# Block 1's first product wholly by seven half products, under a new hand-written order

## The chip, the cores and the metric

The kernel runs on one core of one Trainium2 chip. The metric is the device time of one launch in microseconds (us), lower is better. The core's engines are named as in the profile: PE is TensorE's matrix multiplication and PEld its weight loads, DVE is VectorE, ACT is ScalarE, POOL is GpSimd (here it only issues loads), and SP is SyncE (here it issues transposing DMAs and stores).

## The reference, cut to what matters

Attention with a window feeds a two-layer network. There are 4 batches of 768 tokens, that is 24 tiles of 128 tokens, 8 heads of 64.

```python
scores = scale * q @ k.T + bias            # 96 local keys and 8 global keys are kept
a = softmax(where(keep, scores, -1e9))
x = (a @ v) laid out as 3072 tokens x 512
h = x @ w_in                               # "first product",  512 -> 2048
g = maximum(h, 0) ** 2
out = g @ w_out                            # "second product", 2048 -> 512
```

## The kernel before, in words

The 24 tiles make 12 blocks of two tiles. Tiles 0 and 1 are block 0, tiles 2 and 3 block 1, and so on. For a tile j the program records named operations: the load of q, k and v (`ld.q.j`, `ld.k.j`, `ld.v.j` for the first six tiles, `load.j` later; all issued by POOL in `swdge`, L327), the transposes of q and k on PE (`tr.0.j`, `tr.1.j`) with their copies out of PSUM (`T.0.j`, `T.1.j`), the scores (`sc.j`, after `bias.j` for tiles 0 to 2), the exponentials (`exp.j.odd.g`, ACT), the product with the bias table (`mul.j.g`, DVE), the product with v (`pv.j.half`, PE), its division (`norm.j.half`, two DVE instructions), and the transpose of x (`trx.j` on PE and a copy `xT.j` for tiles 0 to 7, a transposing DMA on SP from tile 8). `gk`, `gv` copy the global keys and values into the tile's own buffers; `gate.j` is a tiny DVE write that a load waits for.

The network's first product for a block has 8 steps of 256 hidden columns. It stands in the program in two forms:

- Plain (`s1.blk.s`, `emit_s1` at L1074): 8 matrix multiplications of 256 columns for one step (in block 0 some steps are cut by token tile or column half), then `relu.blk.s` and `sq.blk.s`.
- By seven half products (`first_seven`, L917; this is the scheme by which a 2x2 block product takes seven block products and some sums, not eight products). Four steps form a group; a group has the products `h.blk.g.p1` to `p7`, each of 8 matrix multiplications of 128 columns. Their operands are parts of `w_in` and of x, sums of parts of `w_in` (`isum.i.g`, four for each group, made once, DVE, L907) and sums of parts of x (`xs.blk.0..2`, DVE, L939). Between products in one PSUM bank the partial results are copied out (`u.blk.g.1..3`). Three of the four quarters of the hidden block come from an addition with relu on DVE (`c.blk.g.c11`, `c12`, `c22`, L1011), and one, `c21`, from a plain relu. Four squares `q.blk.g.*` follow.

The second product goes by seven half products in every block (`s2`, with `sum` and `wsum` on DVE, `part` copies and `o` additions).

Block 0's first product is plain; blocks 2 to 11 go by seven (`SEVEN1`, L280); of block 1 the second group alone goes by seven (`SEVEN1_PART`, L281), and the steps 0 to 3 are plain.

The sums of `w_in` are written over the buffers of the first tiles' q and k (`first_sum`, L238), so each `isum` waits for every transpose and bias product of the tiles 0 to 5 (`first_reads`) and for the four steps of `w_in` that it reads.

Each engine runs its instructions in order. What that order is, and which PSUM bank or buffer each operation takes, is written out by hand in the string `ORDER` (L57), which `Plan.run` (L39) reads word by word: `name:banks`, with `@A` or `@V` where ACT or DVE may do the operation and `#2` for a second one of that name. The order of the loads (words `ld.` and `load.`) is POOL's, that of `T.j` (from tile 8), `xT.j` (from tile 8) and `st` is SP's.

Of the kernel before, what the change touches and what calls it, by code (L numbers as in the profile page):

```python
# [62 lines left out]
trx.1:6 exp.3.0.1 exp.3.1.0:7 exp.3.0.0 ld.win.1.0 pv.2.0:2 pv.2.1:5 norm.2.0:0 norm.2.1 gv.2@V mul.3.0:8 sc.4.0:1037
exp.4.1.0:9 trx.2:2 ld.win.4.0 xT.1@A exp.4.1.1:a tr.1.5:4 tr.0.5:5 T.1.5@A exp.4.0.0 xT.2@A:1 mul.3.1:b pv.3.0:0
pv.3.1:6 T.0.5@A s1.0.1:7 norm.3.0:1 gk.4@V exp.4.0.1 norm.3.1 gv.3@A s1.0.1#2 trx.3:4 sc.5.0:0126 exp.5.0.1:c
exp.5.1.0:d s1.0.4:5 exp.5.1.1 E0.0 mul.4.0:e xT.3@V ld.v.4 mul.4.1:f ones.6 pv.4.0:3 s1.1.1:4 relu.0.4@V:2 exp.5.0.0
ld.win.3.0 s1.0.3:2 pv.4.1:1 relu.0.1@A:0 sq.0.1@A:0 gv.4@A s1.0.3#2 mul.5.1:1 s1.1.3:6 norm.4.0:0 norm.4.1 ld.win.2.0
ld.win.0.0 s1.0.0:5 relu.0.3@A:3 sq.0.3@A mul.5.0:5 gate.10 s1.0.2:0 trx.4:7 relu.1.1@A:4 sq.1.1@A:1 xs.1.0:0 ld.v.5
ld.win.2.1 pv.5.0:3 ld.win.0.1 pv.5.1:1 xs.1.1 ld.win.6.0 ld.win.7.0 ld.win.5.0 relu.1.3@A:7 norm.5.0:1 norm.5.1
ld.wout.3 s1.1.2:2 xT.4@A:2 relu.1.2@A:8 ld.wout.2 ld.wout.1 ld.wout.0 isum.0.0 s1.1.0:4 s1.0.2#2 trx.5:3 gate.14  # L70
xT.5@V relu.1.0@A:6 sq.1.2@A s1.0.0#2 xs.2.0:1 h.2.0.p1:1 sq.1.0@V sq.0.4@A u.2.0.1@A:b isum.3.0 sq.1.3@A xs.2.1
ld.wout.7 isum.0.1 s1.0.0#3 s1.0.6:6 gate.11 isum.1.0 isum.1.1 xs.1.2 s1.0.7:7 h.2.0.p2:2 c.2.0.c11:9 h.2.1.p1:3
relu.0.6@A:a ld.wout.6 ld.wout.5 ld.wout.4 u.2.1.1@A:e relu.0.7@A:c isum.3.1 s1.0.0#4 h.2.1.p5:4 s1.0.2#3 relu.0.0@A:f
h.1.1.p1:6 h.2.1.p2:7 u.1.1.1@A:0 isum.2.1 h.2.1.p6 u.2.1.2@A:d h.1.1.p2:2 c.1.1.c11:3 xs.2.2 c.2.1.c11:5 sq.0.0@A
s1.0.2#4 isum.2.0 h.1.1.p6 u.1.1.2@A:1 h.2.0.p6 u.2.0.2@A:4 h.2.1.p7 u.2.1.3@A:8 h.1.1.p7 h.2.0.p5:5 relu.0.2@A:6
u.1.1.3@A:2 h.2.0.p7 wsum.0.0 h.1.1.p5:2 u.2.0.3@A:7 c.2.1.c22:b wsum.1.0 sq.0.2@A gate.9 s1.0.5:7 h.2.1.p3 wsum.2.0
c.2.0.c22:f load.6 load.7 c.1.1.c22:0 sq.0.7@A relu.0.5@A:e sq.0.6@A sq.0.5@A load.8 c.2.1.c12:8 sum.0.2:0 sum.0.0
h.1.1.p4 h.2.0.p4 wsum.0.1 s2.1.p1.0:0 T.8 c.2.0.c21@A:6 h.2.0.p3 h.2.1.p4 s2.0.p1.0:7 h.1.1.p3 sum.0.1 s2.0.p2.0:4
q.1.1.c22@A q.1.1.c11@A s2.0.p1.1 q.2.1.c22@A:2 q.2.0.c11@A part.0.p1@A:0 c.1.1.c21@A:c s2.0.p2.1 s2.1.p1.1 wsum.1.1
s2.0.p6.0 s2.0.p6.1 c.1.1.c12:7 tr.1.6:1 tr.0.6:6 part.1.p1@A:1 q.1.1.c21@A s2.1.p2.0:2 q.2.1.c11@A sum.0.3 wsum.2.1  # L80
part.0.p6@A:2 o.0.p2:a c.2.1.c21@A:2 s2.1.p2.1 wsum.3.1 wsum.3.0 T.1.6@V s2.0.p7.0 s2.0.p7.1 gate.12 s2.0.p5.0
q.1.1.c12@A s2.0.p5.1 c.2.0.c12:e load.9 part.0.p7@A:3 q.2.1.c12@A T.0.6@A q.2.0.c22@A o.0.p5:d s2.0.p4.0 s2.0.p4.1
q.2.0.c12@A o.0.p4@A sum.1.0:1 s2.0.p3.0 tr.0.7:3 gate.13 sum.1.1 s2.0.p3.1 o.1.p2:0 o.0.p3 sum.1.2 T.0.7@A tr.1.7:1
sum.2.2:0 sum.1.3 sum.2.0 T.1.7@A q.2.0.c21@A s2.1.p6.0 s2.1.p6.1 q.2.1.c21@A part.1.p6@A:0 sc.6.0:567341 exp.6.1.0:3
load.10 gk.7@A exp.6.0.0 s2.1.p5.0 s2.1.p7.0 s2.1.p7.1 mul.6.0:b exp.7.0.0:9 exp.7.1.0 part.1.p7@A:3 s2.2.p1.0:6
s2.1.p5.1 sum.2.1 exp.7.0.1:1 exp.7.1.1 o.1.p5:c mul.7.0:5 s2.2.p1.1 pv.6.0:5 norm.6.0:0 s2.1.p4.0 s2.1.p4.1 o.1.p4@A
pv.6.1:7 s2.1.p3.0 sc.8.0:3415 exp.8.0.1:7 part.2.p1@A:1 pv.7.0:0 s2.1.p3.1 mul.7.1:8 norm.6.1 T.9 pv.7.1:7 norm.7.0:1
norm.7.1 trx.6:1 exp.8.1.0:4 xT.6@V:0 exp.8.1.1 exp.8.0.0 s2.2.p6.0 s2.2.p6.1 o.1.p3 gate.15 trx.7:0 xT.7@A gk.8@V
mul.8.1:f h.3.1.p1:4 u.3.1.1@A:e gv.7@V h.3.0.p2:7 sc.9.0:5132 exp.9.0.1:6 exp.9.1.0:2 xs.3.0:0 xs.3.1 exp.9.0.0
h.3.0.p1:0 h.3.1.p6 mul.8.0:3 s2.2.p2.0:3 u.3.0.1@V:9 pv.8.0:1 u.3.1.2@A:b T.10 c.3.0.c11:1 h.3.0.p6 pv.8.1:5  # L90
norm.8.0:0 exp.9.1.1 sum.2.3 norm.8.1 xs.3.2 part.2.p6@A:2 xT.8:2 s2.2.p2.1 h.3.1.p7 h.3.1.p5:7 u.3.0.2@A:5
u.3.1.3@A:8 c.3.1.c22:7 o.2.p2:4 mul.9.0:3 mul.9.1:9 h.3.0.p7 s2.2.p7.0 s2.2.p7.1 u.3.0.3@A:f q.3.1.c22@A:0
part.2.p7@A:3 q.3.0.c11@A h.3.0.p5:2 h.3.1.p2:1 c.3.1.c11:8 gv.8@V load.11 c.3.0.c22:7 h.3.1.p3 h.3.0.p4 c.3.0.c21@A:2
h.3.1.p4 c.3.1.c21@A:1 q.3.1.c11@A c.3.1.c12:6 s2.2.p5.0 pv.9.0:5 gk.9@V T.11 st.0.0 norm.9.0:1 q.3.1.c12@A
q.3.0.c22@A h.3.0.p3 pv.9.1:1 gv.9@A c.3.0.c12:e norm.9.1 s2.3.p1.0:0 s2.2.p5.1 sc.10.0:4752 exp.10.1.1:f h.4.0.p1:1
s2.2.p4.0 exp.10.1.0:3 s2.2.p4.1 q.3.0.c12@V s2.3.p1.1 sum.3.0:1 o.2.p5:b s2.2.p3.0 s2.2.p3.1 exp.10.0.1 exp.10.0.0
part.3.p1@A:0 sum.3.1 h.4.1.p1:2 s2.3.p6.0 o.2.p4@A mul.10.0:8 s2.3.p6.1 sum.3.2 pv.10.0:7 mul.10.1:9 o.2.p3 gk.10@A
xT.9 norm.10.0:0 xs.4.0:1 xs.4.1 h.4.1.p2:5 pv.10.1:4 q.3.1.c21@A q.3.0.c21@A part.3.p6@A:1 u.4.1.1@A:6 u.4.0.1@A:5
s2.3.p7.0 s2.3.p7.1 h.4.1.p6 u.4.1.2@A:7 norm.10.1 h.4.0.p6 u.4.0.2@A:e gate.18 sc.11.0:6374 exp.11.1.0:a exp.11.0.0
gv.10@V c.4.1.c11:3 part.3.p7@V:3 sum.3.3 xs.4.2 load.12 h.4.0.p2:5 T.12 exp.11.1.1:1 h.4.1.p7 s2.3.p4.0 mul.11.0:2  # L100
exp.11.0.1 c.4.0.c11:f u.4.1.3@A:8 mul.11.1:9 load.13 h.4.0.p7 h.4.1.p5:3 c.4.1.c22:6 s2.3.p2.0:6 pv.11.0:4
u.4.0.3@A:a norm.11.0:1 q.4.1.c11@A:1 h.4.1.p4 h.4.0.p5:7 c.4.0.c22:5 s2.3.p2.1 o.3.p2:2 pv.11.1:5 q.4.1.c22@A
h.4.1.p3 q.4.0.c11@A gate.16 norm.11.1 h.4.0.p4 c.4.1.c21@A:1 c.4.0.c21@A:3 h.4.0.p3 s2.3.p4.1 c.4.1.c12:8 q.4.1.c12@A
c.4.0.c12:6 T.13 s2.3.p5.0 s2.3.p5.1 o.3.p5:9 q.4.0.c22@A q.4.0.c21@A o.3.p4@A sc.12.0:425137 exp.12.0.0:a st.2.1
exp.12.1.0 exp.13.0.0:b exp.13.1.0 exp.13.0.1:f q.4.0.c12@V s2.3.p3.0 sum.4.2:0 sum.4.0 xT.10:1 h.5.1.p1:0 s2.3.p3.1
mul.12.0:7 s2.4.p1.0:4 xT.11 o.3.p3 gate.19 xs.5.0:0 xs.5.1 h.5.0.p1:2 u.5.0.1@A:e q.4.1.c21@A h.5.1.p2:5 s2.4.p1.1
sum.4.1 part.4.p1@A:2 u.5.1.1@A:8 load.15 load.14 st.2.0 st.3.1 h.5.0.p5:1 pv.12.0:6 h.5.0.p6 mul.13.0:5 h.5.0.p2:3
c.5.0.c11:3 norm.12.0:0 s2.4.p6.0 xs.5.2 u.5.0.2@A:6 exp.13.1.1 mul.13.1:a q.5.0.c11@A:2 h.5.1.p6 h.5.0.p7 pv.12.1:7
u.5.0.3@A:4 s2.4.p2.0:3 s2.4.p6.1 s2.4.p2.1 pv.13.0:6 c.5.0.c22:1 gk.13@V h.5.0.p3 u.5.1.2@A:9 c.5.1.c11:b h.5.0.p4
norm.13.0:1 q.5.0.c22@A part.4.p6@A:0 norm.12.1 pv.13.1:5 norm.13.1 o.4.p2:e h.5.1.p7 gate.21 c.5.0.c12:3 h.5.1.p5:6  # L110
s2.4.p7.0 s2.4.p7.1 c.5.0.c21@A:7 q.5.0.c21@A u.5.1.3@A:f load.16 st.1.0 T.14 q.5.1.c11@V c.5.1.c22:0 h.5.1.p4 T.15
sum.4.3 T.16 sc.14.0:7251 xT.12:0 gv.13@A xT.13 q.5.1.c22@V q.5.0.c12@A s2.4.p5.0 part.4.p7@A:3 gate.17 exp.14.1.0:4
# [1337 lines left out]
```

## Time and profile before

| what | value |
|---|---|
| median of 3 runs | 197.52 us (197.02 to 198.58) |
| the profiled execution | 197.45 us, of which 195.7 us from the first to the last instruction |
| granted TensorE clock | 1.000 |
| busiest engines after PE | DVE 92%, ACT 83% of the span |

The profiled execution is one run. "Span" is the time between its first and last instruction; 1.75 us of its own time lie around the span. In the views below a row gives a start and a duration in us, the engine, the line of the kernel, and output<-input by the program's names; in brackets stands the idle time of the engine before it and what ended that. In the table by stretches a column gives busy time and, in parentheses, instructions. Groups give total busy us and the mean ns of one instruction; the duration of a matrix multiplication or of a vector instruction holds its latency too, so the distance between the starts of two neighbours is shorter.

### The profile page before, as it was taken

The numbers are of one execution on the slowest core, as the hardware profiler recorded it, in microseconds if no ns is written. First come the engines' busy times: TensorE is split into PE (matmuls) and PEld (weight loads), VectorE is DVE, ScalarE is ACT, GpSimd is POOL, SyncE is SP. The second block draws the span as 40 slices with busy tenths as digits, with TensorE's granted clock in tenths as the row PEclk, the third lists the DMA queues.
The fourth block names the chain that finished last, engine by engine and source line by source line (L and its number), as shares of the span: only waits on it lengthen the run. The fifth ranks groups of instructions, "written<-read, shape, count | busy, mean of one in ns | idle before, by whom it ended". The sixth has DMA issues, their size and how long they took to land.

```text
span 195.7 us, 6835 instructions
## 1 busy us (share of the span) xinstructions
PE 188.5 (96%) x2808; PEld 170.5 (87%) x2808; DVE 179.4 (92%) x437; ACT 161.6 (83%) x338; POOL 75.1 (38%) x93
## 2 busy tenths in 40 slices
...
GB/s 125 149 150 167 179 193 205 205 162 151 155 150 143 99 177 168 119 100 227 139 79 129 138 74 119 209 168 97 147 113 188 85 136 13 20 193 105 0 91 234
DMA packets 111713, 26.92 MB, mean 138 GB/s; under 512 B 103234, under 2 KB 108866, under 8 KB 111682
## 3 DMA queue, kind: packets, MB, share of 16 engines
...
q14 instruction: 9, 0.07, 0.1%
...
## 4 chain that ended last, share of the span: by engine, by line
PE 85%; POOL 6%; DMA 5%; DVE 1%; issue 0%; POOLq 0%; DVEq 0%
PE bank L1230 37%; PE bank L967 32%; PE bank L1081 6%; PE bank L618 5%; PE bank L767 5%; POOL qk_first L330 5%; DMA win<-in_moe_w_in_dram 3%; DMA xT<-x 2%; POOL v L330 2%; PE bank L835 1%; PE bank L528 0%; DVE xs L939 0%; DVE buf L886 0%; DVE hsum L1185 0%; DVE early L1305 0%
## 5 line engine op out<-in xcount | busy, mean ns | idle before, releaser
L684 ACT ACTIVATE buf<-bank 128x512 bf16<-128x512 f32 x76 | 41.5, 613 | 2.8 <-PE bank L618 2.7
L1031 ACT ACTIVATE hs<-buf 128x512 bf16<-128x512 f32 x62 | 37.2, 635 | 2.5 <-DVE buf L1011 2.0
L1230 PEld LDWEIGHTS <-hsum 128*128 128x128 bf16 x384 | 35.3, 98 | 4.0
L453 ACT COPY buf<-bank 128x512 f32<-128x512 f32 (+1 forms) x59 | 32.1, 569 | 7.7 <-PE bank L967 6.1
L1230 PE MATMUL bank<-wsum,hsum 128*128 128x256 bf16 x288 | 38.0, 273 | 0.0
L1011 DVE CUSTOM_DVE_ANT_0 buf<-bank,buf 128x512 f32<-128x512 f32 x49 | 33.0, 682 | 0.8 <-ACT buf L453 0.3
L967 PEld LDWEIGHTS <-qk_first 128*128 128x128 bf16 x504 | 31.1, 98 | 1.4 <-issue 0.3
L967 PEld LDWEIGHTS <-win 128*128 128x128 bf16 x504 | 30.8, 98 | 0.9
L334 POOL DMA_DIRECT2D qk<-in_q_dram x18 | 16.0, 889 | 35.3 <-DMA qkT<-qk 30.0
L1230 PEld LDWEIGHTS <-hs 128*128 128x128 bf16 x288 | 26.3, 98 | 2.7
L1230 PE MATMUL bank<-wout,hs 128*128 128x256 bf16 x192 | 27.3, 273 | 0.0
L334 POOL DMA_DIRECT2D v<-in_v_dram x18 | 16.0, 891 | 23.1 <-PE bank L967 13.1
L967 PE MATMUL bank<-xs,qk_first 128*128 128x128 bf16 x336 | 24.6, 219 | 0.2 <-DVE buf L886 0.2
L967 PE MATMUL bank<-xT,win 128*128 128x128 bf16 x336 | 24.6, 219 | 0.0
L709 DVE TENSOR_TENSOR buf<-buf,E 128x1024 bf16<-128x1024 bf16 x32 | 21.5, 683 | 0.5 <-ACT buf L684 0.5
L798 DVE TENSOR_TENSOR x<-bank,rs 128x256 bf16<-128x256 f32 x48 | 20.4, 425 | 1.7
L767 PE MATMUL bank<-v,buf 128*128 128x65 bf16 x312 | 16.1, 193 | 0.9 <-DMA v<-in_v_dram 0.5
L1185 DVE TENSOR_TENSOR hsum<-hs 128x1024 bf16<-128x1024 bf16 (+1 forms) x26 | 16.4, 642 | 0.3
L334 POOL DMA_DIRECT2D qk<-in_k_dram x18 | 16.1, 897 | 0.6 <-DMA wout<-in_moe_w_out_dram 0.4
L767 PEld LDWEIGHTS <-buf 128*128 128x128 bf16 x312 | 13.9, 98 | 1.8 <-DVE buf L709 0.6
L884 ACT ACTIVATE buf<-bank 128x512 f32<-128x512 f32 x23 | 13.7, 607 | 1.0 <-PE bank L967 1.0
L453 ACT COPY part<-bank 128x256 f32<-128x256 f32 x29 | 11.1, 383 | 3.6 <-PE bank L1230 3.6
...
## 6 DMA issues: line engine op xcount, KB each, us to landing
...
```

Of the source, the lines that this page charges most:

```text
L334: nc.gpsimd.dma_start(out=dst, in_=src)
L453: nc.scalar.copy(dst, src)
L684: nc.scalar.activation(out=tiles[tag, j, g][:, odd], in_=tiles.pop(("sc", j, odd, g)).rearrange("p a c -> p (a c)"), func=Act.Exp, scale=s ...
L709: nc.vector.tensor_mul(at, tiles.pop(("esc", j, g)), bias)
L767: nc.tensor.matmul(out=po[:, hi, :], lhsT=tiles["at", j, g][:, odd, at * P : (at + 1) * P], rhs=v_sb[kj][:, h, :], start=(i == 0), stop=(i ...
L798: nc.vector.tensor_tensor(out=x[:, 4 * hf : 4 * hf + 4, :], in0=po[:, :, :D], in1=rs.to_broadcast([P, 4, D]), op=Alu.mult,)
L884: nc.scalar.activation(dst, src, Act.Relu)
L967: nc.tensor.matmul(out=tiles["h", blk, g, bank][:, n], lhsT=left_[:, s, k], rhs=right_[:, k], start=opens and n == 0 and k == 0, stop=k == ...
L1011: nc.vector._custom_dve(TENSOR_ADD_SAT, out=hr, in0=src, in1=tiles.pop(("u", blk, g, i)), s0=float("inf"), s1=0.0,)
L1031: nc.scalar.activation(hs, hr, Act.Square)
L1185: nc.vector.tensor_tensor(out=t[:, i, h], in0=t[:, a, h] if isinstance(a, int) else half_a(blk, *a)[:, h], in1=t[:, b, h] if isinstance(b, ...
L1230: nc.tensor.matmul(out=tiles["acc", blk, bank][:, cols], lhsT=left_[:, s], rhs=right_[:, cols], start=first and s == 0, stop=s == NSTEP - ...
```

## The change

Block 1 is put into `SEVEN1`, and the half-way form goes. Block 1's four plain steps `s1.1.0` to `s1.1.3` with their `relu` and `sq` become the group `h.1.0.p1` to `p7` with its copies `u.1.0.*`, its `c.1.0.*` and `q.1.0.*`. `ORDER` is a new one from its first word to its last, with other banks, other choices between ACT and DVE, and another order of the loads.

```diff
-    SEVEN1 = set(range(2, NBLK))
-    SEVEN1_PART = {(1, 1)}
+    SEVEN1 = set(range(1, NBLK))
...
-    def first_seven(blk, groups=(0, 1)):
-        husers = hs_users.setdefault(blk, [])
+    def first_seven(blk):
+        husers = hs_users[blk] = []
...
-        for g in groups:
-            group(g)
+        group(0)
+        group(1)
...
-        if (blk, s // GRP) in SEVEN1_PART:
-            if s % GRP == 0:
-                first_seven(blk, (s // GRP,))
-            continue
```

The words of `ORDER` on which the prediction rests, cut to the engine named (before, then after):

```
POOL before: ld.q.1 ld.k.1 ld.q.2 ld.k.2 ld.q.3 ld.v.0 ld.k.3 ld.v.1 ld.k.4 ld.q.4 ld.v.2 ld.q.5 ld.k.5 ld.v.3
             ld.win.1.0 ld.win.4.0 ld.v.4 ld.win.3.0 ld.win.2.0 ld.win.0.0 ld.v.5 ld.win.2.1 ld.win.0.1
             ld.win.6.0 ld.win.7.0 ld.win.5.0 ld.wout.3 ...
POOL after:  ld.k.1 ld.q.1 ld.v.1 ld.k.2 ld.q.2 ld.v.0 ld.q.4 ld.k.3 ld.win.4.0 ld.q.3 ld.v.2 ld.k.4 ld.v.3 ld.q.5 ld.k.5
             ld.win.0.0 ld.v.4 ld.win.1.0 ld.win.3.0 ld.win.0.1 ld.win.2.0 ld.win.2.1 ld.v.5
             ld.win.6.0 ld.win.7.0 ld.win.5.0 ld.wout.1 ...
PE before:   ... pv.3.0 pv.3.1 s1.0.1 s1.0.1#2 trx.3 sc.5.0 s1.0.4 pv.4.0 s1.1.1 s1.0.3 pv.4.1 s1.0.3#2 s1.1.3
             s1.0.0 s1.0.2 trx.4 pv.5.0 pv.5.1 s1.1.2 s1.1.0 s1.0.2#2 trx.5 s1.0.0#2 h.2.0.p1 ...
PE after:    ... tr.0.3 pv.1.1 trx.0 sc.3.0 tr.1.4 trx.1 pv.2.0 pv.2.1 sc.4.0 s1.0.4 tr.0.5 pv.3.0 tr.1.5 pv.3.1
             trx.2 s1.0.0 sc.5.0 trx.3 s1.0.1 s1.0.1#2 pv.4.0 pv.4.1 s1.0.3 s1.0.3#2 s1.0.0#2 s1.0.0#3 trx.4
             s1.0.0#4 s1.0.2 h.1.0.p1 h.1.0.p2 h.1.0.p5 pv.5.0 h.1.0.p6 pv.5.1 s1.0.6 h.1.0.p7 h.2.0.p2 trx.5 ...
DVE after:   ... T.1.4 xT.1 norm.2.0 mul.3.0 mul.3.1 norm.2.1 norm.3.0 T.0.5 T.1.5 norm.3.1 mul.4.1 gv.3 mul.4.0
             xs.1.0 xs.1.1 norm.4.0 norm.4.1 mul.5.0 gv.4 isum.0.0 isum.1.0 mul.5.1 norm.5.0 isum.3.0 xs.1.2 norm.5.1 ...
```

By the words of the two orders DVE does 3 more additions with relu (`c`), 3 more of the copies `u`, and 8 fewer others (one `c21`, one `relu`, one `sq`, one `q`, two `o.p4`, one `part`, one `gk`); ACT does 5 more in all; the loads, stores and transposing DMAs are the same ones in another order.

More of the change, by code (lines that the diff above doesn't have):

```diff
@@ L63 @@
[L63 to L112, printed above, removed]
@@ new lines @@
+s2.0.p5.0 tr.1.7:5 tr.0.7:0 s2.0.p5.1 q.2.1.c21@A part.0.p7@A:3 q.2.0.c21@A gate.10 T.1.7@A wsum.3.0 sum.1.0:1
+s2.0.p4.0 s2.0.p4.1 o.0.p5:9 q.2.1.c12@A sum.1.1 s2.0.p3.0 o.1.p2:4 T.1.6@V s2.0.p3.1 q.2.0.c22@A o.0.p4@A T.0.7@A
+s2.1.p6.0 s2.1.p6.1 q.2.0.c12@A o.0.p3 q.2.1.c11@A part.1.p6@A:0 sum.1.2 sc.6.0:152607 sum.2.0:0 s2.1.p5.0 sum.1.3
+s2.1.p7.0 s2.1.p7.1 gate.14 sum.2.2 exp.6.1.0:5 s2.2.p1.0:5 s2.1.p5.1 exp.6.0.0 sum.2.1 mul.6.0:c exp.7.1.0:b
+part.1.p7@A:3 s2.1.p4.0 exp.7.0.0 gk.7@A load.10 load.11 o.1.p5:d pv.6.1:1 pv.6.0:6 s2.1.p4.1 mul.7.0:f norm.6.0:0
@@ new lines @@
+h.4.1.p1:3 load.13 T.13 pv.10.0:6 c.3.1.c21@A:1 part.3.p1@A:0 s2.3.p6.0 h.4.0.p2:0 s2.3.p6.1 u.4.0.1@A:b sum.3.2
+u.4.1.1@A:e exp.10.1.1:3 h.4.1.p2:4 xs.4.0:0 q.3.1.c21@A norm.10.0:0 xs.4.1 gk.10@V h.4.1.p6 q.3.0.c21@A o.2.p3
+c.4.1.c11:6 exp.10.0.1 mul.10.1:0 h.4.0.p6 sc.11.0:6254 u.4.1.2@A:2 u.4.0.2@A:f h.4.1.p7 h.4.0.p7 load.14
+part.3.p6@A:1 xs.4.2 c.4.0.c11:c pv.10.1:0 exp.11.1.0:1 sum.3.3 exp.11.1.1:5 norm.10.1 exp.11.0.1 u.4.1.3@A:e
+mul.11.1:3 exp.11.0.0 h.4.0.p5:2 s2.3.p7.0 u.4.0.3@A:b h.4.1.p5:4 h.4.1.p4 c.4.1.c21@A:0 s2.3.p2.0:5 c.4.1.c22:5
```

167 lines of the change are left out of this document (105 added, 62 removed).

## The prediction, made before the changed kernel ran

> **What bounds the kernel now.** I read the page first (busy shares, the 40 slices), then the table by stretches, the chain of waits in time, and last the PE, POOL and DVE rows of the first 30 us.
>
> ```profile
> span 195.7 us, 6835 instructions
> PE 188.5 (96%) x2808; PEld 170.5 (87%) x2808; DVE 179.4 (92%) x437; ACT 161.6 (83%) x338; POOL 75.1 (38%) x93
> ```
> ```profile
> 25.00:30.00 5.00, 5.00 (x77) 4.74 (x76) 4.06 (x14) 4.94 (x11) 3.63 (x6) 1.00 1.49 199
> 30.00:60.00 30.00, 30.00 (x420) 27.69 (x419) 29.41 (x65) 28.09 (x61) 19.73 (x24) 1.00 1.92 170
> 60.00:183.00 123.00, 122.81 (x1926) 113.75 (x1924) 117.65 (x272) 105.22 (x220) 28.88 (x33) 1.00 1.07 125
> ```
> ```profile
> 13.60 6.01 DMA win<-in_moe_w_in_dram
> ...
> 19.66 1.07 PE bank L1081 x16
> ...
> 33.39 1.79 PE bank L967 x32
> ...
> 38.52 0.87 PE bank L1081 x8
> ```
>
> The columns of the table are the stretch, its length, then busy us of PE, PEld, DVE, ACT and POOL. From 25 to 183 us PE is idle for 0.19 us, and from 19.66 on the chain is PE's own work almost alone. What the chain shows ahead of it is the load of the first `w_in` step, issued at 13.60 and landed at 19.61. So the time is what PE loses before about 20 us, plus the PE work, plus a tail. DVE stands right behind: 29.41 of 30 us between 30 and 60. The change can act in three places: the PE work, the loss at the start, and the places where DVE is level with PE.
>
> **The change part by part.** *PE work.* Out go 4 plain steps, in come 7 half products. From the chain, 32 multiplications of 128 columns take 1.79 us, so one half product of 8 takes 0.447; 8 multiplications of 256 columns (one step) take 0.87. That is 7 x 0.447 - 4 x 0.87 = 3.13 - 3.48 = -0.35 us, all of it on the path, because PE does not wait there.
>
> Against that price speaks another row, the weight load that each of them needs:
>
> ```profile
> L967 PEld LDWEIGHTS <-win 128*128 128x128 bf16 x504 | 30.8, 98 | 0.9
> ```
>
> A load takes 98 ns; hidden behind the work before it, it costs nothing, and 1.79 us for 32 pairs (56 ns each) says that it is hidden. Unhidden, 56 of them take 5.5 us, which is +2.0 and not -0.35; the row of 1.79 decides, and the other end stays as a rival below.
>
> The Trainium skill, "TensorE: Matmul & The Clock Gate", section "Back-to-back issue gap", speaks for that rival: in a real stream of weight loads and multiplications, it says, one of 128 columns costs about 81 ns and not the isolated 56. By it the seven products would take 56 x 81 ns = 4.5 us, an estimate, and the sum would be 200.2. This case's row, 56 ns, disagrees.
>
> *DVE and ACT work.* Prices:
>
> ```profile
> L1011 DVE CUSTOM_DVE_ANT_0 buf<-bank,buf 128x512 f32<-128x512 f32 x49 | 33.0, 682 | 0.8 <-ACT buf L453 0.3 <-PE bank L967 0.3
> L886 DVE TENSOR_SCALAR early<-bank 128x512 f32<-128x512 f32 x2 | 1.4, 688 | 0.0
> L455 DVE COPY part<-bank 128x256 f32<-128x256 f32 x7 | 2.9, 415 | 0.1
> L1031 ACT ACTIVATE hs<-buf 128x512 bf16<-128x512 f32 x62 | 37.2, 635 | 2.5 <-DVE buf L1011 2.0
> ```
>
> DVE gains three additions (0.68) and three copies (as L886, 0.69), 4.1 us; it loses a `c21`, `relu`, `sq` and `q` (as large, 2.7 together), two `o.p4` and a `part` (0.415 each) and a `gk` (less than that), about 4.2 us. ACT gains 5 operations net, 2 to 3 us at 0.635 or less, against 34 us of idle time. Neither total moves the end. What moves is when DVE has to do it: three additions and the four `isum` of the first group now stand inside the first 37 us.
>
> *The start.* POOL issues the loads in another order, and they land in that order.
>
> ```profile
> 10.14 0.97 POOL L330 DMA_DIRECT2D v<-in_v_dram  x1
> 11.00 0.98 POOL L330 DMA_DIRECT2D qk_first<-in_q_dram  x1
> ...
> 13.60 1.62 POOL L330 DMA_DIRECT2D win<-in_moe_w_in_dram  x2
> ...
> 21.25 1.57 POOL L330 DMA_DIRECT2D win<-in_moe_w_in_dram  x2 [0.53 <-DMA win<-in_moe_w_in_dram]
> 23.43 0.74 POOL L330 DMA_DIRECT2D win<-in_moe_w_in_dram  x1 [0.62 <-DMA win<-in_moe_w_in_dram]
> 25.17 2.82 POOL L330 DMA_DIRECT2D wout<-in_moe_w_out_dram  x4 [0.29 <-DMA win<-in_moe_w_in_dram]
> ```
> ```profile
> 14.16 0.39 PE L528 MATMUL bank<-ident,qk_first 128*128 128x128 bf16 x4
> ...
> 15.77 0.65 PE L767 MATMUL bank<-v,buf 128*128 128x65 bf16 x16 [0.49 <-DMA v<-in_v_dram]
> ...
> 22.32 0.41 PE L767 MATMUL bank<-v,buf 128*128 128x65 bf16 x8
> ```
> ```profile
> 14.30 0.17 DVE L797 RECIPROCAL rs<-bank 128x4 f32<-128x4 f32 x1
> 14.51 0.42 DVE L798 TENSOR_TENSOR x<-bank,rs 128x256 bf16<-128x256 f32 x1
> 14.85 0.75 DVE L455 COPY qkT<-bank 128x512 bf16<-128x512 bf16 x2
> ...
> 17.32 0.41 DVE L455 COPY v<-v 8x520 bf16<-8x520 bf16 x1
> 17.65 1.27 DVE L709 TENSOR_TENSOR buf<-buf,E 128x1024 bf16<-128x1024 bf16 x2
> ...
> 27.67 0.68 DVE L907 TENSOR_TENSOR qk_first<-win 128x1024 bf16<-128x1024 bf16 x1
> ```
>
> The 11th load (`v.2`, issued at 10.14) lands at about 15.7, when `pv.2` starts after waiting for it; the 15th (`win.1`) at 19.6. POOL keeps eight loads under way, so its waits show later landings: the 24th issue waits for the 16th load, the 26th for the 18th, the 28th for the 20th. Between the first two (one small, one whole step of `w_in`) lie 2.18 us, between the next (two half steps) 1.74. That makes 0.86 for a q, k, v or half step and 1.32 for a whole step. After the change the 9th load is a whole step of `w_in`, so `k.4`, the 12th, lands at 15.7 + 0.86 + (1.32 - 0.86) = 17.0. Before, `k.4` was the 9th load.
>
> `tr.1.4` waits for it on PE (0.39 with its latency), so its copy `T.1.4` starts on DVE at about 17.5. In the new DVE order 12 operations follow before `pv.4.0` can start. Distances between starts, from the rows above: copies 0.35, a `norm` 0.55, a `mul` 0.60, a `gv` 0.33. Sum from `T.1.4` to the end of `mul.4.0`: four copies (`T.1.4`, `xT.1`, `T.0.5`, `T.1.5`) 1.4, four `norm` 2.2, four `mul` 2.4 + 0.07 latency, one `gv` 0.33 = 6.4. So `pv.4.0` starts at 17.5 + 6.4 + 0.1 = 24.0. `win.1`, now the 18th load, lands at 19.6 + 2 x 0.86 + 1.32 = 22.6, and two steps' halves (2 x 0.447) follow it: 23.5. DVE ends last, by half a microsecond. ACT's exponentials for tile 4 are due before that.
>
> Before, `pv.4.0` starts at 22.32. PE has then done the same transposes, scores, products with v, `s1.0.1` and `s1.0.4`; the changed kernel has one quarter of `s1.0.0` (0.22) in addition. The start is late by 24.0 - 22.32 - 0.22 = 1.46 us, and as PE is never idle later, that is not caught up. Bounds: 0.5 if the landings run 1 us ahead of these sums, 2.0 if `mul.4.1` waits for ACT as well.
>
> *The `isum`.* The first starts at 27.67 before. Now the last piece of the steps 0 to 3 is the 22nd load, with `v.5` behind it, so it lands 0.86 earlier, by about 26.6. DVE gets there at 23.9 + 0.55 (two `xs`) + 1.1 + 0.6 + 0.35 = 26.5 and ends the first `isum` at 27.2; PE wants `h.1.0.p5` at about 27.4. Cost nothing, cover 0.2; each later us counts in full, as `p6`, `p7` and everything of block 2 stand behind it on PE.
>
> *Level stretch.* In 30 to 60 us DVE idled 0.59 us before, hidden by its lead on PE. That lead is now about as large as PE's new delay leaves it, with the `isum` moved ahead. Bounds 0 and 0.59; I take 0.25.
>
> *SP and POOL later.*
>
> ```profile
> qkT<-qk SPq DMA_TRANSPOSE x16, 5.2
> xT<-x SPq DMA_TRANSPOSE x16, 2.7
> ```
>
> In SP's order `T.23` now stands behind `xT.21`, which waits for `norm.21`; PE has 7.6 us of its own work between that and `sc.23`, SP needs 1.2 for `xT.21` and 5.2 for the landing. Cost nothing, cover about 1 us. The loads 12 to 23 keep their gates and slots. `xs.7` has 3.9 us of DVE work behind `norm.15` against 2.7 for the transposed x. Cost nothing. The last products of block 11 stand in the same order, so the tail stays.
>
> **Sum**, against the profiled execution of 197.45 (span 195.7 and 1.75 around it; the median of the runs is 197.52): 197.45 - 0.35 + 1.46 + 0.25 = 198.8, that is +0.7%. About 1% is what a measurement of this kernel can tell from no change, so this counts as the same.
>
> **The rivals.** *The start costs nothing.* For it: the new order has a step of `w_in` landed by about 13.5 and begins the first product with `s1.0.4` at about 18.6, against 19.66. If the loads are not bound by rate this early, the whole step in 9th place delays nothing, and -0.35 stays, perhaps with another 0.4 of the small waits gone: 196.7 to 197.1. Against it: loads are issued 0.86 apart and land 0.86 apart, with no slack to take 0.46. *DVE becomes the bound until 60 us* (the other side). If `isum.0.0` starts later than 26.7, PE waits at `h.1.0.p5`, and each idle time of DVE until block 3 is passed on. Price: 0.59 in full and 0.9 for a `w_in` piece as late as before (27.67 against 26.7): 198.8 + 0.35 + 0.9 = 200.1. Against it: one load less stands ahead of the piece. *The weight loads of block 1's narrow multiplications are not hidden* (98 ns in place of 56): 198.8 + 0.35 + 2.0 = 201.2. Against it: the same instructions ran at 56 in the chain.
>
> **How the numbers follow.** Chances: forecast 0.60; start for nothing 0.18; DVE the bound 0.19; weight loads in the open 0.03. The range takes the low bound of the start and the rival beside it (197.45 - 0.35 + 0.5 = 197.6, down to 197.1) and reaches to the DVE rival: 197.1 to 200.1. Faster than 195.5 would need more than all waits gone: 0.03. Slower than 199.5: the two slow cases, 0.22, less a little for their low ends, plus the forecast's upper end: 0.21. Same: 0.76.
>
> **What would show it.** `pv.4.0` (L767 x8) starts at 24.0 and DVE idles just before a copy at 17.5 behind L528: the start is right; at 22.6 it is wrong. `tr.1.4` at 17.0: the load rate is right. `h.1.0.p1` at about 26.5, no wait of PE for L907: the `isum` are covered. L967 in steps of 0.45 for 8, with 56 more of them than before: the PE term. DVE busy above 29.5 in 30 to 60 with PE waits for DVE rows there: the level stretch. A median under 197 or over 200.1 would make the prediction wrong.

## The result, and the profile after

The changed kernel takes 199.22 us (median of 20 executions, 198.66 to 200.88), the kernel before 197.50 beside it (20 executions, 196.99 to 199.51): ratio 1.0081, 95% interval 1.0057 to 1.0105. So it is slower by 0.8%, which is under the 1% that was called no change. The profiled execution took 199.33 with a span of 197.6; before these were 197.45 and 195.7. The span grew by 1.9, where the sum of the prediction had 1.36.

Where it went is read from the busy times by stretch. The columns are the stretch, then its length, then the busy time of PE, PEld, DVE, ACT and POOL (with their instructions), the granted clock, the DMA share and GB/s. The changed kernel:

```profile
30.00:60.00 30.00, 30.00 (x424) 27.74 (x422) 29.50 (x64) 29.07 (x63) 18.74 (x23) 1.00 1.84 170
60.00:90.00 30.00, 30.00 (x487) 27.76 (x486) 28.28 (x66) 27.75 (x59) 11.13 (x13) 1.00 1.34 109
90.00:108.00 18.00, 16.93 (x264) 15.40 (x262) 15.72 (x41) 14.94 (x34) 6.14 (x7) 1.00 1.72 190
108.00:183.00 75.00, 75.00 (x1171) 70.08 (x1169) 70.73 (x160) 63.80 (x131) 12.26 (x14) 1.00 0.90 105
```

The kernel before, in the last two of these stretches:

```profile
90.00:108.00 18.00, 18.00 (x296) 16.56 (x293) 17.29 (x45) 16.74 (x37) 6.14 (x7) 1.00 1.30 138
108.00:183.00 75.00, 74.81 (x1153) 69.71 (x1150) 71.51 (x160) 61.92 (x129) 12.25 (x14) 1.00 0.88 117
```

PE never idles from 30 to 90 and from 108 to 183. In 90 to 108, where it had no gap before, it now idles 1.07. The rest must lie in the start. There, the timeline of the changed kernel (start, us, engine, line, operation, count, and in brackets the idle time before it and what ended that) has:

```profile
14.84 0.40 PE L528 MATMUL bank<-ident,qk_first 128*128 128x128 bf16 x4 [1.00 <-DMA qk_first<-in_q_dram]
16.71 0.40 PE L528 MATMUL bank<-ident,qk_first 128*128 128x128 bf16 x4 [0.33 <-DMA qk_first<-in_k_dram]
17.14 0.50 DVE L455 COPY qkT<-bank 128x512 bf16<-128x512 bf16 x1
22.75 0.67 DVE L709 TENSOR_TENSOR buf<-buf,E 128x1024 bf16<-128x1024 bf16 x1
23.48 0.66 PE L767 MATMUL bank<-v,buf 128*128 128x65 bf16 x16
25.92 0.67 DVE L907 TENSOR_TENSOR qk_first<-win 128x1024 bf16<-128x1024 bf16 x1
25.99 1.06 PE L967 MATMUL bank<-xT,win 128*128 128x128 bf16 x16
26.89 0.33 PE L967 MATMUL bank<-xs,qk_first 128*128 128x128 bf16 x3
```

These are `tr.0.3`, `tr.1.4`, its copy `T.1.4`, `mul.4.0`, `pv.4.0`, the first `isum`, `h.1.0.p1` with `p2`, and the head of `p5`. `k.4`, on which `tr.1.4` waits, is in the chain of waits with its issue and its time to landing:

```profile
10.91 5.75 DMA qk_first<-in_k_dram
```

`pv.4.0` stands at 23.48, so the start is late by 23.48 - 22.32 - 0.22 = 0.94.

The two gaps in 90 to 108 have the same look. First PE, then ACT, then the last of the stores in the chain of waits, from its issue to its landing at 98.93:

```profile
95.10 0.41 PE L767 MATMUL bank<-v,buf 128*128 128x65 bf16 x8
95.34 0.61 PE L967 MATMUL bank<-xs,win 128*128 128x128 bf16 x8
95.79 0.41 PE L767 MATMUL bank<-v,early 128*128 128x65 bf16 x8
96.74 0.61 PE L967 MATMUL bank<-xs,win 128*128 128x128 bf16 x8 [0.54 <-ACT buf L453]
...
100.92 0.61 PE L967 MATMUL bank<-xT,qk_first 128*128 128x128 bf16 x8
102.06 0.60 PE L1228 MATMUL bank<-wsum,hs 128*128 128x256 bf16 x4 [0.53 <-ACT part L453]
```
```profile
94.14 0.59 ACT L453 COPY buf<-bank 128x512 f32<-128x512 f32 x1
96.10 0.59 ACT L453 COPY buf<-bank 128x512 f32<-128x512 f32 x1 [1.38 <-DMA out_dram<-buf]
...
99.01 0.60 ACT L884 ACTIVATE buf<-bank 128x512 f32<-128x512 f32 x1 [1.03 <-DMA out_dram<-buf]
```
```profile
92.68 6.25 DMA out_dram<-buf
```

ACT wants to write a buffer and waits until a store has read it: the output sums lie in the same ring of 16 buffers (`buf` and `early` in the views) as the copies `u` and the relus. A group of 8 with v takes 0.24 (95.10 to 95.34), so the work at 96.74 was due at 96.03; a group of 8 of L967 takes 0.44, so that at 102.06 was due at 101.36. The two waits cost PE 0.71 + 0.70 = 1.4, more than the idle time beside their rows, because the next instruction starts before the last has ended when nothing is waited for.

Why the stores are late is in SP's row, that is the transfers in the order in which SP issues them, of the kernel before and of the changed one:

```profile
77.65 8.07 SPq L859 DMA_TRANSPOSE xT<-x  x2
85.78 1.61 SPq L1327 DMA_DIRECT2D out_dram<-buf  x2
87.48 0.41 SPq L1327 DMA_DIRECT2D out_dram<-early  x1
88.00 8.10 SPq L554 DMA_TRANSPOSE qkT<-qk  x3
96.20 3.03 SPq L859 DMA_TRANSPOSE xT<-x  x2
```
```profile
80.60 7.06 SPq L859 DMA_TRANSPOSE xT<-x  x2
87.77 3.16 SPq L554 DMA_TRANSPOSE qkT<-qk  x2
91.03 2.10 SPq L1325 DMA_DIRECT2D out_dram<-buf  x3
94.39 1.21 SPq L859 DMA_TRANSPOSE xT<-x  x1
```

Before, the stores go ahead of the transposing transfers `T.14` to `T.16`. In the new order `T.14` and `T.15` come first, the stores are issued at 91.0 to 93.1, and the last lands at 98.93. The profiled loss closes with this: 0.94 (start) + 1.40 (two waits) - 0.35 (PE's products) - 0.19 (a gap of the kernel before, 75.00 - 74.81, that is gone) = 1.80, against 1.9.

### The profile page after: what moved, and what is told of

It is laid out like the page before. It is cut to its first block, busy times and chain, and to the rows that moved or that the text cites. A ratio compares the mean times of both kernels' runs of the same rounds, so it can differ in the third digit from the quotient of the medians.

```text
span 197.6 us, 6908 instructions
## 1 busy us (share of the span) xinstructions
PE 188.4 (95%) x2832; PEld 171.0 (87%) x2832; DVE 177.5 (90%) x435; ACT 163.6 (83%) x343; POOL 75.3 (38%) x93
## 4 chain that ended last, share of the span: by engine, by line
PE 83%; DMA 6%; POOL 5%; ACT 2%; DVE 2%; issue 1%; SPq 0%; POOLq 0%; ACTq 0%
PE bank L1228 36%; PE bank L967 33%; PE bank L767 5%; PE bank L618 5%; POOL qk_first L330 3%; DMA out_dram<-buf 3%; PE bank L1077 3%; DMA qk_first<-in_k_dram 3%; POOL v L330 1%; PE bank L528 1%; PE bank L835 1%; DVE buf L709 1%; ACT hs L1031 1%; ACT buf L684 1%; POOL win L330 0%
## 5 line engine op out<-in xcount | busy, mean ns | idle before, releaser
L684 ACT ACTIVATE buf<-bank 128x512 bf16<-128x512 f32 x70 | 39.1, 615 | 3.2 <-PE bank L618 3.2
L453 ACT COPY buf<-bank 128x512 f32<-128x512 f32 (+1 forms) x60 | 32.7, 559 | 10.2 <-PE bank L967 5.7
L1228 PE MATMUL bank<-wsum,hsum 128*128 128x256 bf16 x288 | 39.8, 273 | 0.0
L1228 PEld LDWEIGHTS <-hsum 128*128 128x128 bf16 x384 | 35.2, 98 | 4.1
L967 PEld LDWEIGHTS <-win 128*128 128x128 bf16 x528 | 32.8, 98 | 1.5 <-issue 0.6
L967 PEld LDWEIGHTS <-qk_first 128*128 128x128 bf16 x528 | 32.5, 98 | 0.7
L1011 DVE CUSTOM_DVE_ANT_0 buf<-bank,buf 128x512 f32<-128x512 f32 x44 | 29.8, 686 | 2.1 <-PE bank L967 0.9
L1228 PEld LDWEIGHTS <-hs 128*128 128x128 bf16 x288 | 26.6, 98 | 3.7 <-issue 0.7
L1228 PE MATMUL bank<-wout,hs 128*128 128x256 bf16 x192 | 27.5, 273 | 0.0
L967 PE MATMUL bank<-xs,qk_first 128*128 128x128 bf16 x352 | 25.9, 219 | 0.0
L967 PE MATMUL bank<-xT,win 128*128 128x128 bf16 x352 | 25.6, 219 | 0.0
L1303 DVE TENSOR_TENSOR buf<-bank,part 128x256 f32<-128x256 f32 x29 | 12.2, 421 | 5.0 <-PE bank L1228 2.5
L453 ACT COPY part<-bank 128x256 f32<-128x256 f32 x30 | 11.8, 395 | 4.4 <-PE bank L1228 4.4
L884 ACT ACTIVATE buf<-bank 128x512 f32<-128x512 f32 x20 | 12.3, 621 | 2.6 <-PE bank L967 1.5
L709 DVE TENSOR_TENSOR buf<-buf,E 128x1024 bf16<-128x1024 bf16 x21 | 14.1, 684 | 0.1
L1228 PE MATMUL bank<-wsum,hs 128*128 128x256 bf16 x96 | 13.6, 273 | 0.5 <-ACT part L453 0.5
```

The source lines that it names most:

```text
L453: nc.scalar.copy(dst, src)
L684: nc.scalar.activation(out=tiles[tag, j, g][:, odd], in_=tiles.pop(("sc", j, odd, g)).rearrange("p a c -> p (a c)"), func=Act.Exp, scale=s ...
L709: nc.vector.tensor_mul(at, tiles.pop(("esc", j, g)), bias)
L884: nc.scalar.activation(dst, src, Act.Relu)
L967: nc.tensor.matmul(out=tiles["h", blk, g, bank][:, n], lhsT=left_[:, s, k], rhs=right_[:, k], start=opens and n == 0 and k == 0, stop=k == ...
L1011: nc.vector._custom_dve(TENSOR_ADD_SAT, out=hr, in0=src, in1=tiles.pop(("u", blk, g, i)), s0=float("inf"), s1=0.0,)
```

## The experiments

Two theories were tested. One: the loss in 90 to 108 comes from three stores that stand behind two transposing transfers on SP. Its rivals: ACT is late there anyway, or the transfers become the wait when they are put back. Two: the start is held by landings, `win.4` (`ld.win.4.0`, a whole step of `w_in`) above all; its rival is DVE's chain. A third question was what the seven products themselves do. All edits are in the string `ORDER`; only the runs with the group plain again also take `SEVEN1` and `first_seven` of the kernel before. A ratio is to the kernel before on the same chip, with its 95% interval; it is not the quotient of the two medians.

**The stores first.**

```diff
-exp.13.0.0:c T.14 h.5.1.p2:7 ... T.15 ... h.5.0.p6 st.1.1 st.3.1 st.2.0 part.4.p1@A:2
+exp.13.0.0:c st.1.1 st.3.1 st.2.0 T.14 h.5.1.p2:7 ... T.15 ... h.5.0.p6 part.4.p1@A:2
```

> The changed kernel with one thing undone: on SP the three stores st.1.1, st.3.1 and st.2.0 go ahead of the transposing transfers T.14 and T.15, as stores did before the change. Nothing else is moved on any engine. Theory (the stores, issued at 91.0 to 93.2 behind T.14 and T.15, land at 96.0 to 98.9 and hold the buffers that ACT wants at 94.7 and 98.0): they are issued from about 87.8 and land by about 94, ACT waits for none of them, PE's two waits for ACT of 0.54 and 0.53 at 96.7 and 102.1 go, and the time falls by 1.0 to 1.3, from 199.2 to about 198.0. Rival 1 (ACT and DVE are late there with or without the stores, as they also carry block 1's smaller products): the waits for the stores shrink, PE waits for ACT all the same, 199.0 to 199.3. Rival 2 (T.14 and T.15, now 2 us later, become the wait): PE waits for the scores of tile 14, L618, by 0.5 to 1.5 near 105, and the time stays at 198.7 to 199.7.

Measured: 198.82 (8 executions), ratio 1.0063 (1.0038 to 1.0088). Both waits at 97 and 102 are gone, and no engine waits for a store in 88 to 108. But there is a new one:

```profile
99.57 1.30 SPq L859 DMA_TRANSPOSE xT<-x  x1
```
```profile
99.57 5.47 DMA xT<-x
...
105.13 0.42 DVE xs L939
```
```profile
106.76 0.61 PE L967 MATMUL bank<-xT,win 128*128 128x128 bf16 x8 [0.66 <-DVE x L798]
```

`xT.13` is now the last of a full row of SP. It is issued at 99.57, though its x was ready earlier (the last norm of tile 13 ends at 97.7 in the changed kernel). DVE waits in `xs.6` for its landing, `norm.14` stands behind that, and PE behind the norm. So the theory's mechanism is right, and in this execution rival 2 is right in kind, though with another transfer: what is taken from the stores is asked of the next. It need not be so each time. The run of both edits below has the same row on SP; there `xT.13` was issued at 98.91 and landed 4.3 us later, and PE has no gap in 90 to 108.

**The stores and `xT.13` first** (called the repaired kernel from here on). As above, and:

```diff
-xT.12:0 ... T.16 st.1.0 ... norm.13.1 h.5.0.p3 ... xT.13 sum.5.0:1
+xT.12:0 ... st.1.0 ... norm.13.1 xT.13 T.16 h.5.0.p3 ... sum.5.0:1
```

> The changed kernel with the three stores ahead of T.14 and T.15 on SP as before, and one step more: xT.13, the transposed transfer of x that stood last in SP's row of 80 to 101 us, goes ahead of T.16. Theory (with the stores first, xT.13 was issued at 99.57, 1.9 after norm.13 was done, landed at 105.0, and DVE and then PE waited for it: 0.66 at 106.8): it is issued at about 97.7, lands by 103.3, that wait goes as well, and the time is 198.82 - 0.66 = 198.1. T.16 lands 1.3 later than in the changed kernel, near 105, and its scores are wanted after 110, so nothing waits for it. Rival (it is the DMA queues, filled by the transposing transfers between 88 and 100, that hold everything up, whatever the order): xT.13 lands 1 us earlier at most and the wait shrinks to 0.2 to 0.5, or T.16 becomes the wait: 198.5 to 198.9.

Measured: 198.62 (12 executions, 197.81 to 199.48), ratio 1.0041 (1.0014 to 1.0067); the profiled execution 198.10. The median lies where the rival had it, the profiled execution and its rows where the theory had them: `xT.13` is issued at 97.77, and PE has no gap left in the stretch:

```profile
90.00:108.00 18.00, 18.00 (x294) 16.55 (x293) 17.18 (x44) 16.02 (x37) 6.13 (x7) 1.00 1.65 190
108.00:183.00 75.00, 75.00 (x1156) 70.07 (x1154) 70.16 (x159) 64.06 (x133) 12.25 (x14) 1.00 0.88 105
```

PE runs the same instructions in the same order here as in the changed kernel, so the two products that waited there, at 96.74 and 102.06, can be set beside their rows here:

```profile
96.07 0.61 PE L967 MATMUL bank<-xs,win 128*128 128x128 bf16 x8
...
100.69 0.60 PE L1228 MATMUL bank<-wsum,hs 128*128 128x256 bf16 x4
```

They come 0.67 and 1.37 earlier, which bears out the 1.40 above for this pair of executions. The account closes without the stores: the start is late by 23.57 - 22.32 - 0.22 = 1.03, less 0.35 and less the 0.19, which makes 0.49; the span is 196.3 against 195.7.

**The same two kernels once more, side by side.**

> The changed kernel once more, beside the next one on the same chip. Theory (the late stores cost PE two waits, at about 97 and 102): both waits stand in this profile too, 0.4 to 0.7 each, with ACT's waits for the stores' landing ahead of them, and the time is 0.7 to 1.2 above that of the next kernel. Rival (the two waits were an accident of one execution): they are missing here, or the two times agree within 0.3.

> The kernel with the stores and xT.13 first on SP once more. Theory: no wait of PE over 0.2 between 90 and 108, 198.3 to 198.6, and 0.7 to 1.2 under the kernel before this one in the list. What is left over the kernel before the change, 0.6 to 1.0, is the start (1.0 later) less PE's 0.35. Rival (SP's row matters by chance only): within 0.3 of the changed kernel.

Measured: 199.00, ratio 1.0055 (1.0024 to 1.0087), for the changed kernel, and 198.92, ratio 1.0074 (1.0042 to 1.0106), for the repaired one (12 executions each). By the times that is the rival: they are the same. By the traces it is half of each. The changed kernel again waits for a store, with one gap on PE that the profile lists, not two (its waits between 88 and 108):

```profile
ACT buf L884 <- DMA out_dram<-buf: 0.9, 1, 0.9
...
PE bank L1228 <- ACT part L453: 0.4, 1, 0.4
```

By distances, as above, the gap costs 0.55 (the product ahead of it starts at 102.17, so the next was due at 102.61 and starts at 103.16), and a delay of 0.19 stands at the place of the other one: 0.74. The repaired one has none there (PE busy 18.00 of 18.00), but idles 0.14 after 108, and that is a store again, the next one. It is issued at 108.42 and lands 4.2 later, and DVE, whose relu wants its buffer, waits:

```profile
112.70 0.69 DVE L1011 CUSTOM_DVE_ANT_0 buf<-bank,buf 128x512 f32<-128x512 f32 x1 [0.48 <-DMA out_dram<-buf]
```

So it goes in all five traces with this row on SP and the seven products (three are of runs below): DVE waits there 0.34 to 0.94. What it costs PE is read from the product of L1228 with `wout` and `hs` ahead of that place (in this trace at 113.14) to the next of L1228 (115.12): 1.98 here, 1.77 or 1.78 in five traces in which DVE does not wait there, and 1.84 in the repaired kernel's first execution. So this store cost 0.07 there and 0.21 here; the repair has moved a part of the wait to the store behind. All in all, an engine waits for a store between 88 and 108 in four of the five traces with the changed kernel's row on SP (both of the changed kernel, the run with `win.4` later and the second with the group plain; the first with the group plain has no such wait), and in that stretch in none of the eight with the stores first. That the late stores hold ACT, and ACT holds PE, is shown. The price is not fixed: 1.40 and about 0.7 in two executions of the same kernel. The medians of all executions differ by 0.34 only (199.17 of 32 against 198.83 of 24), and with the overlap of the intervals above that is not told from nothing.

**The whole step of `w_in` later.**

```diff
-ld.k.3 ld.win.4.0 ld.q.3 ... ld.v.2 ld.k.4 ld.v.3
+ld.k.3 ld.q.3 ... ld.v.2 ld.k.4 ld.win.4.0 ld.v.3
```

> The changed kernel with one load moved back: the whole step of w_in (ld.win.4.0), 9th on POOL's queue, goes behind ld.k.4, so that it is the 12th and q.3, v.2 and k.4 are the 9th to 11th. Nothing else is moved. Theory (the start is paced by landings, 1.32 us for a whole step against 0.86 for the others): q.3 lands at 13.5 in place of 14.8 and k.4 at 15.3 in place of 16.7, the step itself at 16.7, before s1.0.4 wants it at 18.3. PE's waits for q.3 (1.00) and k.4 (0.33) go and DVE's chain of copies, norms and muls starts earlier by up to 0.7, until win.1, which lands at 22.1 as before, holds s1.0.1: pv.4.0 at about 23.0 to 23.2 in place of 23.48, time 198.7 to 198.9. Rival (the chain on DVE and ACT itself, exponentials included, sets 23.4): pv.4.0 stays within 0.1 of 23.48, time 199.2.

Measured: 199.62 (6 executions), ratio 1.0113 (1.0080 to 1.0146). No gain. The wait has moved to `win.1`, right behind which `pv.4.0` comes no earlier than before the edit:

```profile
22.65 1.07 PE L1077 MATMUL bank<-xT,win 128*128 128x128 bf16 x16 [0.60 <-DMA win<-in_moe_w_in_dram]
23.55 0.65 PE L767 MATMUL bank<-v,buf 128*128 128x65 bf16 x16
```

The theory named `win.1` as the limit, but at 22.1, not 22.6, and so was too hopeful. This trace has PE's two gaps too (0.48 at 96.97 and 0.37 at 102.14). For the second the profile names a store; ahead of the first ACT's copy starts at 96.34, when the first store, issued at 91.40, has just landed 4.9 us later, though the profile names PE.

**Both edits.**

> The changed kernel with both moves: the three stores ahead of T.14 and T.15 on SP, and the whole step of w_in behind k.4 on POOL. If both theories hold the gains add, as they lie in stretches in which PE is the bound between them: 199.2 - 1.15 - 0.4 = 197.65, level with the kernel before at 197.5. If only the stores matter, 198.0; if only the load, 198.8; if neither, 199.2.

Measured: 198.47 (12 executions), ratio 1.0059 (1.0033 to 1.0086): what the stores give, and nothing from the load that the times can show. In its trace `pv.4.0` stands at 23.23, again right behind a wait for `win.1`.

**Three more tries at the start.** With the stores and `xT.13` first: two loads moved, `win.4` behind `k.4` as above and `win.1` a place forward, ahead of `v.4`; or the copy `xT.0` moved from DVE to ACT (`xT.0@V:0` to `xT.0@A:0`); or both.

> As the run before, with the start's loads put in another order too: the whole step of w_in (win.4) behind k.4, and win.1, on which the chain of waits of the run with only win.4 moved hung (issued 18th, landed at 22.3 to 22.6, s1.0.1 right behind it), one place forward, ahead of v.4. Theory: win.1 lands about 0.86 earlier, at 21.5; then DVE's last mul for tile 4, which ended at 22.9 to 23.0 in those runs, sets pv.4.0: 22.9 to 23.1 against 23.48, and the time is 198.1 - 0.4 = 197.7, level with the kernel before or within 0.2 of it. Rival (v.4, a place later, or the exponentials set it): pv.4.0 at 23.3 to 23.6 and 198.1.

> The changed kernel with the stores and xT.13 first on SP, and one copy of the start moved: xT.0, at 16.7 on DVE, goes to ACT, which idles from 15.9 to 16.6 for the scores of tile 3. Theory (from 15.3 on the start hangs on DVE, which runs without a gap from T.0.3 to the last mul of tile 4): DVE's chain loses one copy of 0.34, unless T.1.4 then waits for k.4, which lands at 16.7 with the loads in this order and leaves 0.1 to 0.2 of it: pv.4.0 0.1 to 0.34 earlier, 23.2 to 23.4, time 198.3 to 198.5. Rival (the landings alone set it): pv.4.0 at 23.5 to 23.6, 198.6.

> As the run before with the start's loads reordered too (win.4 behind k.4, win.1 ahead of v.4), which alone gave nothing. Theory: with both out of the way, k.4 by 15.8 to 16.9 and DVE's chain shorter by a copy, pv.4.0 comes to 22.9 to 23.2, time 198.0 to 198.2. Rival (the start is held by how fast the loads land in all, not by their order): s1.0.1 and s1.0.3 wait for win.1 and win.3 instead, pv.4.0 at 23.3 or later, 198.6 to 198.9.

Measured: 198.87, 198.90 and 198.82 (12 executions each); ratios 1.0037 (1.0006 to 1.0068), 1.0062 (1.0030 to 1.0095) and 1.0070 (1.0040 to 1.0101). With the loads alone `pv.4.0` stood at 24.00: PE had waited 1.0 for `k.4`, which landed later in this execution, though issued a place earlier, than in the changed kernel. With the copy alone it came to 23.09, 0.48 earlier than in the repaired kernel. That looks like DVE's theory, and is not. `tr.1.4`, which starts when `k.4` has landed, and `pv.4.0` in the repaired kernel, then with the copy alone (PE):

```profile
16.79 0.40 PE L528 MATMUL bank<-ident,qk_first 128*128 128x128 bf16 x4 [0.20 <-DMA qk_first<-in_k_dram]
...
23.57 0.66 PE L767 MATMUL bank<-v,buf 128*128 128x65 bf16 x16
```
```profile
16.39 0.40 PE L528 MATMUL bank<-ident,qk_first 128*128 128x128 bf16 x4 [0.57 <-DMA qk_first<-in_k_dram]
...
23.09 0.66 PE L767 MATMUL bank<-v,buf 128*128 128x65 bf16 x16
```

`k.4` happened to land 0.40 earlier; from `tr.1.4` to `pv.4.0` it takes 6.78 and 6.70, so the copy itself gave 0.08. With both edits PE waited for `win` twice, here and at 24.53 (0.36):

```profile
22.62 1.07 PE L1077 MATMUL bank<-xT,win 128*128 128x128 bf16 x16 [0.70 <-DMA win<-in_moe_w_in_dram]
23.52 0.65 PE L767 MATMUL bank<-v,buf 128*128 128x65 bf16 x16
```

So two landings bound the start. One is that of `k.4`, with a chain behind it whose length hardly changes: in the seven traces with the changed kernel's start and the full clock `tr.1.4` stands at 16.23 to 16.86, and `pv.4.0` 6.77 or 6.78 later in each. The other is that of `win.1`: in the three traces in which PE waits for it, `pv.4.0` comes 0.90 after that wait (23.55, 23.23, 23.52). The two end within half a microsecond of each other, and either shows when the other comes earlier. The 0.48 did not reach the end: PE idles 0.35 after 108 in that execution (74.65 of 75.00), where the repaired kernel had none, and the time is 198.90. Of the 0.43 that were left of it at 55, none is left at 66.4, with no wait of PE that the profile lists. Then it is the next store again, in the chain that ended last:

```profile
108.65 4.05 DMA out_dram<-buf
```

DVE's L1011 waits 0.94 until 112.83. Between the two products of L1228 it takes 2.43, so 0.66 more than without the wait; with the loads alone and with both edits it was 2.27 and 2.17, so 0.50 and 0.40. So the times of these three tries do not show what their starts gave.

**The group plain again in the new order.** Four plain steps in the places of the seven products, three times; the diff is that of the second. The third has SP's row as repaired above and the squares `sq.1.2` and `sq.1.3` earlier, right behind `sq.1.1` and `relu.0.7`.

```diff
-h.1.0.p1:2 u.1.0.1@A:2 h.1.0.p2:0 ... h.1.0.p5:3 ... h.1.0.p6 ... u.1.0.2@A:7 ... h.1.0.p7 ... c.1.0.c11:8 ... u.1.0.3@A:b
+s1.1.0:2 relu.1.0@A:2 s1.1.1:0 ... s1.1.2:3 ... relu.1.1@A:7 ... relu.1.2@A:3
...
-h.1.0.p4 ... c.1.0.c22:e ... q.1.0.c11@A:1 ... h.1.0.p3 ... c.1.0.c12:5 c.1.0.c21@A:3 q.1.0.c22@A ... q.1.0.c21@A ... q.1.0.c12@A
+s1.1.3:2 ... sq.1.0@A:1 ... relu.1.3@A:5 sq.1.1@A ... sq.1.2@A ... sq.1.3@A
```

> The new order without the change: block 1's first half product is computed plainly again, four steps s1.1.0 to s1.1.3 with a relu and a square each, set in the new order at the places of its seven products and their sums; loads, transfers and all the rest stand as in the changed kernel. The output is the same function. Theory (the seven products save 4 x 0.87 - 7 x 0.447 = 0.35 on PE, and the rest of the loss lies in the order): the waits at the start and at 96 and 102 stay, and the time is 199.2 + 0.35 = 199.55. Rival 1 (the work that the seven products put on DVE and ACT costs PE something between 25 and 60 us or feeds the waits at 96): the time falls, to 198.0 to 199.0. Rival 2 (narrow multiplications do not hide their weight loads): it falls by 1.6, to 197.6.

> The new order without the change, with the work of ACT kept one for one: block 1's first half product is plain again (four steps, 0.87 each on PE), its four relus at the places of the three copies and the one relu of the seven-product form, its four squares at the places of the other squares; DVE has three sums less. The function computed is the same. Theory (the seven products save 0.35 on PE, all the rest of the loss lies in the order, the waits for the stores at 96 and 102 among it): 199.2 + 0.35 = 199.55, pv.4.0 at 23.5 and the two waits as in the changed kernel. Rival 1 (the sums on DVE cost PE something between 25 and 60 us): the time falls, to 198.5 to 199.1. Rival 2 (PE's narrow multiplications cost more than 56 ns each): 197.6 to 198.5.

> Block 1's first half product plain again in the new order, with two things mended against the run before of this kind: SP's row is the one with the stores and xT.13 first, so that the waits of 96 to 107 us are out of the comparison, and the last two of the four squares stand earlier on ACT, so that PE does not wait for them at 42 and 43 (1.7 us there). To be compared with the run of the seven products with the same SP row (198.62, its last product starting at 192.77). Theory (the seven products save 4 x 0.87 - 7 x 0.447 = 0.35 on PE, their sums on DVE and ACT cost it nothing): 199.0, last product 0.35 later after the start is taken out. Rival 1 (their work on DVE and ACT costs PE more than 0.35 between 25 and 60): 198.0 to 198.6. Rival 2 (the plain form's squares, wanted all at once by block 1's second product, hold PE up even so): 199.3 or more with waits of PE for L1117.

Measured: 204.09 (6 executions), ratio 1.0302 (1.0261 to 1.0343); 200.70 (6), ratio 1.0124 (1.0092 to 1.0157); 199.57 (9), ratio 1.0098 (1.0061 to 1.0134). In the first of the three two squares read buffers that had been written again, so part of block 1's hidden values are others, and PE idles 2.3 in one wait for ACT's copy (L453); it tells nothing of the change. In the second PE waits 1.4 for the squares (L1117), which the plain form wants earlier than the places of the seven-product form give them. The third, against the repaired kernel with the same SP row, is the usable one. Its stretch from 30 to 60:

```profile
30.00:60.00 30.00, 29.39 (x409) 27.05 (x407) 27.56 (x59) 28.49 (x62) 19.17 (x23) 1.00 1.80 164
```

Its span is 197.1 against 196.3. What the products make of that can be read between two points of PE's order that both kernels have, `pv.4.0` (at 23.57 with the seven products, at 23.40 with the plain steps) and `tr.0.6`. The repaired kernel, then the plain one:

```profile
45.68 0.61 PE L528 MATMUL bank<-ident,qk 128*128 128x128 bf16 x8
```
```profile
37.39 0.61 PE L967 MATMUL bank<-xs,plain 128*128 128x128 bf16 x8 [0.23 <-ACT early L453]
...
46.25 0.61 PE L528 MATMUL bank<-ident,qk 128*128 128x128 bf16 x8
```

That is 22.11 with the seven products and 22.85 with the plain steps, 0.74 more. The one wait in between, at 37.39, costs 0.40 of it (the product ahead starts at 36.55, so this one was due at 36.99), and 0.34 is left for the products, against 0.35 forecast. A second wait follows at 47.24, 0.38 of idle time for DVE's L1150; with the first it makes the 0.61 that PE idles in this stretch. So the seven products are no burden in their new order: taking them out made it slower, by the term expected and by waits in the makeshift places. The rivals that would have made it faster fell. The second rival of the last run has the time, 199.3 or more, but not the reason: PE does not wait for the squares (L1117) there.

No version tried beats the kernel before.

## Why the prediction was right, point by point, and where it was not

It said 198.8 and no change by the 1% bound; it is 199.22. That the total came so near is in part luck, because two errors partly cancelled: the start and the level stretch were put 0.77 too high together, and the waits for the stores, 1.40 in the profiled execution, at nothing.

- **PE's products, -0.35.** Right as far as it can be seen: a pair of products at 25.99 takes 0.90 to the next at 26.89, so 0.45 each, and the plain form took 0.34 more between the two points above. The rival of weight loads in the open is out: this trace has 0.45 / 8 = 56 ns for each multiplication. The Trainium skill, "TensorE: Matmul & The Clock Gate", section "Back-to-back issue gap", gives about 81 ns for such a multiplication in a stream. This trace does not agree, and the measurement decides.
- **The start, +1.46.** The direction and the chain were right, the size was not: 0.94. The step "`k.4`, the 12th, lands at 17.0" failed by 0.34: issued at 10.91, it landed at 16.66. It was built on the 11th load's landing at 15.7 before, and by its landing events the 11th came at 15.7 in the changed kernel too, in spite of the whole step ahead of it. From `T.1.4` to `pv.4.0` it took 6.34, against 6.5 forecast. In seven traces with this start at full clock `pv.4.0` stood at 23.01 to 23.63, six of them at 23.40 or later, so 0.9 to 1.1 is the usual price against the one trace of the kernel before. That the chain hangs on `k.4` is borne out by all seven: the distance from `tr.1.4` is the same, only the landing differs.
- **The level stretch, +0.25.** Wrong: 0. DVE is busy 29.50 of 30, and PE 30.00. Its small idle times stayed covered.
- **The `isum`, nothing.** Right: the first starts at 25.92, 0.8 ahead of what was forecast as needed, and PE waits for none.
- **SP and POOL later, nothing.** Here the prediction failed. It walked through `T.23` and `xs.7` and did not ask about the stores, which had moved behind `T.14` and `T.15`. It counted what waits for the transfers, and not what waits for the stores: the buffer that each must read before ACT may write it. That cost 1.40 in the profiled execution and about 0.7 in the other one.
- **The rival that DVE becomes the bound** did not come: PE has no wait for DVE between 27 and 90.

Open is how much of the 0.8% the stores make in an average execution (the repaired kernel, which still waits for one, is 0.3 us faster by the medians; in two traces of the changed one they cost 0.7 and 1.4), and how the start could be had back: moving loads so that `k.4` came earlier uncovered `win.1`.
